# Joining the small matmuls behind z's sums, loading wo's last rows ahead of M's stores, and one normalisation behind an output block

## The chip, the cores and the metric

The kernel runs on one core of a Trainium2 chip. Five engines work side by side: TensorE (PE in the profile, its weight loads PEld), VectorE (DVE), ScalarE (ACT), GpSimd (POOL) and SyncE (SP), which here issues the DMAs. The metric is the device time of one execution in microseconds (us), as the median of repeated runs. For this kernel it was 301.76 us over three runs (301.67 to 302.19).

## The reference

The program mixes two blocks by a gate. Block A is a long convolution of the input along the sequence plus a skip term; block B is linear attention.

```python
x = A_u
g = _sigmoid((x * gate_w).sum(-1, keepdims=True))
a = _A_ref(x, A_A_re, A_A_im, A_B_re, A_B_im, A_C_re, A_C_im, A_log_dt, A_Dskip)
b = _B_ref(x, B_wqkv, B_wo)
return g * a + (1 - g) * b
```

Block B, with 32 heads of 20 channels, 2048 positions and 640 channels:

```python
phi = lambda t: jnp.where(t > 0, t + 1, jnp.exp(t)) + 1e-6
pq, pk = phi(q), phi(k)
kv = jnp.einsum("bhsd,bhse->bhde", pk, v)
z = jnp.einsum("bhsd->bhd", pk)
num = jnp.einsum("bhqd,bhde->bhqe", pq, kv)
den = jnp.einsum("bhqd,bhd->bhq", pq, z)[..., None] + 1e-6
o = num / den
return (lambda x, *d: x.transpose(*d))(o, 0, 2, 1, 3).reshape(B, S, D) @ wo
```

## The kernel before, in words

Each large product is made of three matmuls: an operand is split into a high part (`hi`, a copy on ScalarE) and a low part (`lo`, a subtraction on VectorE), and high by high, low by high and high by low are summed in PSUM (`mm3`).

**First stage (to about 146 us).** For 16 tiles of 128 positions the kernel computes k, its phi, the running sum `zacc`, and the product G = x^T phi(k), which is kept transposed in `GT` in five blocks of columns. Columns 512 to 640 come out turned the other way round, in the tile `rem`: two halves of 320 columns, copied out of PSUM at lines 610 (ScalarE) and 611 (VectorE).

**Second stage.** Everything here stands in the order of the string `PLAN`, read word by word by the loop at the end of `body`; each engine runs its instructions in the order in which they are written. The words are:

- `q`: one block of q for 512 positions and 128 channels, 15 matmuls into a PSUM tile `qp`, then exp, relu, phi (`qe`) and the denominator's running sum `acc` (`q_block`). Four groups of 512 positions have five blocks each.
- `z`: the denominator's constants (`z_const`, PSUM tile `cp`) and the gate's row (`gates_row`, PSUM tile `gp`).
- `kv0` to `kv2`: kv of a pair of head groups (a group has 120 channels, six heads) out of `GT` and the weights `Wv` (`kv_mm`, PSUM tile `kvps`). VectorE masks it into `kvT`, one of two tiles `kvz` that the pairs take in turn.
- `m0` to `m2`: M = kv times wo of a pair (`m_mm`, PSUM tiles `mps`), split into `Mgh` and `Mgl` and stored to DRAM. `ml` loads all of M back, reordered.
- `d`: the denominator of a group (`q_den`: PSUM tile `dp`, then a reciprocal).
- `n`: one block of q normalised (`q_norm`): VectorE multiplies `qe` by the denominator `d`; the high and low parts `pTh` and `pTl` follow with the next `flush`.
- `f`: one output block (`final_mm`: 15 matmuls into a PSUM tile `fp`; `final_out`: VectorE adds the convolution's part `yb` into `o`, which is stored). A `y_block` follows: a load of `yb`, or its computation, and a product with the gate on GpSimd.
- `c`: one convolution block (`conv_out`).

`z_part` (z's sums out of `zacc`, PSUM tile `zp`) stands ahead of the string. The five transposes of `rem` into `GT` (`rem_out`, PSUM tiles `tp`) stand behind the first `q`.

PSUM has eight banks: three with the tag `q`, three with the tag `f` (taken in turn by `kvps`, half of `mps`, `dp` and `fp`), two with the tag `m`. A tile is written anew only when its former content has been read. In SBUF the raw rows of `wo` of the groups 3 and 4 share the tag `wo`, with two slots; the last group's 40 rows (`wo_load(NB)`) take the slot of group 3, which is free when M of pair 1 has been computed. That load is asked for behind `m_mm(1)`, and so behind the eight stores of M that `m_mm(1)` issues on SyncE.

Of the kernel before, what the change touches and what calls it, by code (L numbers as in the profile page):

```python
# [30 lines left out]
F32 = mybir.dt.float32  # L31
# [8 lines left out]
P = 128  # L40
L = 2048
D = 640
NB = D // P
# [18 lines left out]


PLAN = """
q0 kv0 q0 z q0 m0 kv1 q0 c q0 m1 kv2
q1 d0 q1 m2 ml n0 q1 n0 n0 q1 n0 y q1 n0
q2 q2 y q2 d1 n1 f q2 n1 y f q2 n1 n1 f n1 f
q3 f q3 d2 n2 f q3 n2 f q3 n2 n2 f q3 n2 f
f d3 n3 f n3 n3 f n3 f n3 f
f f f f f f  # L70
"""
# [3 lines left out]
def f32(ap):  # L75
    return ap.bitcast(F32)


def body(tc, i, outT):
    nc = tc.nc  # L80
    pe, act, dve, pool, sp = nc.tensor, nc.scalar, nc.vector, nc.gpsimd, nc.sync
    outer, top, kst = ExitStack(), ExitStack(), ExitStack()

    def mk(stack, name, space=None):
        kw = {} if space is None else {"space": space}
        if space is not DRAM:
            kw["reuse_waits"] = "tile"
        return stack.enter_context(tc.tile_pool(name=name, bufs=1, **kw))
# [10 lines left out]
    def hi(dst, src):  # L99
        act.activation(dst, src, AF.Copy)  # L100

    def lo(dst, src, h, eng=None):
        (eng or dve).tensor_tensor(dst, src, f32(h), op=OP.subtract)  # L103
# [6 lines left out]
    def col(tag, n=NB, dt=F32):  # L110
        return pc.tile([P, n], dt, tag=tag, name=tag)
# [25 lines left out]
    s_all = col("s_all", NT)  # L137
    ident = col("ident", P)
    bdm = col("bdm", HC)
    kvz = [col(f"kvT{k}", P) for k in range(2)]  # L140
    for v in kvz:
        pool.memset(v, 0.0)
    dtc, k0, dsk, lam, ok = [col(n) for n in ("dtc", "k0", "dsk", "lam", "ok")]
# [74 lines left out]
    gps = {}  # L218
# [26 lines left out]
    def g_out(b, eng):  # L245
        src = gps.pop(b)
        (hi if eng is act else dve.tensor_copy)(GT[:, b, :512], src)


    kvs, wos = {}, {}  # L250


    def parts(gi):
        c0, n = GRP[gi]
        return [(r, c0 + o, min(HC, n - o)) for r, o in ((0, 0), (64, HC)) if o < n]

    def wo_load(gi):
        tag, nb = ("st", 3) if gi in (0, 1, 2) else ("wo", 2)
        w = wos[gi] = pw.tile([P, D + 2], F32, tag=tag, bufs=nb, name="wo")
        for r, c, n in parts(gi):  # L260
            m = min(64, D - c) if r == 0 else n
            sp.dma_start(w[r : r + m, :D], i["wo"][c : c + m, :])
# [3 lines left out]
    def out_row(gi, r):  # L266
        return r if gi % 2 == 0 else 64 - r

    def kv_mm(pr):
        p = pqp.tile([P, 512], F32, tag="f", bufs=3, name="kvps")  # L270
        kvT = kvs[pr] = kvz[pr % 2]
        for k, gi in enumerate((2 * pr, 2 * pr + 1)):
            for b in range(NB):
                for r, c, n in parts(gi):
                    pe.matmul(p[r : r + n, k * 64 : k * 64 + n], Wv[:, b, c : c + n], GT[:, b, c : c + n],
                              start=(b == 0), stop=(b == NB - 1))
        for k, gi in enumerate((2 * pr, 2 * pr + 1)):
            for r, c, n in parts(gi):
                o = out_row(gi, r)
                dve.tensor_tensor(kvT[r : r + n, o : o + n], p[r : r + n, k * 64 : k * 64 + n], bdm[r : r + n, :n],  # L280
                                  op=OP.mult)

    def m_mm(pr):
        kvT = kvs.pop(pr)
        both = 2 * pr, 2 * pr + 1
        ps = {}
        for hf in range(2):
            for gi in both:
                ps[gi, hf] = mbank("mps") if hf == 0 else pqp.tile([P, 512], F32, tag="f", bufs=3, name="mps")
            for gi in both:  # L290
                for r, c, n in parts(gi):
                    o = out_row(gi, r)
                    pe.matmul(ps[gi, hf][o : o + 64, :320], kvT[r : r + n, o : o + 64],
                              wos[gi][r : r + n, hf * 320 : hf * 320 + 320], start=True, stop=True,
                              tile_position=(r, o))
        for gi in both:
            wos.pop(gi)
            rows = slice(0 if len(parts(gi)) == 2 else out_row(gi, 0), P)
            h = pq.tile([P, D], F32R, tag="so", bufs=2, name="Mgh")
            l = pw.tile([P, D + 2], F32R, tag="st", bufs=3, name="Mgl")  # L300
            for hf in range(2):
                sl = slice(hf * 320, hf * 320 + 320)
                hi(h[rows, sl], ps[gi, hf][rows, :320])
                lo(l[rows, sl], ps[gi, hf][rows, :320], h[rows, sl])
            for v, to in ((h, M_d[0]), (l, M_d[1])):
                for r, c, m in parts(gi):
                    o = out_row(gi, r)
                    sp.dma_start(to[c : c + m, :], f32(v[o : o + m, :D]))
# [8 lines left out]
    def gates_row():  # L317
        gp = mbank("gp")
        pe.transpose(gp[:NT, :P], g, ident)
        gr = pc.tile([NT, P], F32, tag="gr", name="gr")  # L320
        dve.tensor_copy(gr, gp[:NT, :P])
        sp.dma_start(g_d, gr)
        for gi in range(NG):
            gb_load(gi)

    def z_part():

        zp = mbank("zp")
        for b in range(NB):
            pe.matmul(zp[:, b : b + 1], zacc[:, b * P : b * P + P], ones[:, :1], start=True, stop=True)  # L330
        dve.tensor_scalar(zc, zp[:, :NB], float(L) * EPS, None, op0=OP.add)
        dve.tensor_reduce(zs, zc, axis=AX.X, op=OP.add)
        z2 = zs.to_broadcast([P, 2])
        hi(zsh, z2)
        lo(zsl, z2, zsh)

    def z_const():
        cp = mbank("cp")
        pe.matmul(cp[:, :2], bm, zsh, start=True, stop=False)
        pe.matmul(cp[:, :2], bm, zsl, start=False, stop=True)  # L340
        dve.tensor_scalar(ch, cp[:, :1], EPS, EPS, op0=OP.mult, op1=OP.add)
# [60 lines left out]
    def u_load(j):  # L402
        gi, b = divmod(j, NB)
        if j < NK or j >= NS:
            us[j] = pw.tile([P, D + 2], F32, tag="st", bufs=3, name="u")
        else:
            us[j] = pq.tile([P, 512], F32, tag="u", bufs=1, name="u")
        sp.dma_start(us[j][:, :512], i["xT"][b * P : b * P + P, gi * 512 : gi * 512 + 512])
# [199 lines left out]
    g_main(NT - 1, (3, 4))  # L608
    rem = col("rem", D)
    hi(rem[:, :320], gps.pop(("r", 0))[:, :320])  # L610
    dve.tensor_copy(rem[:, 320:], gps.pop(("r", 1))[:, :320])
    g_out(3, act)
    g_out(4, dve)
    kst.close()
# [3 lines left out]
    pqp = mk(top, "pqp", PSUM)  # L618

    def mbank(name):  # L620
        return pqp.tile([P, 512], F32, tag="m", bufs=2, name=name)

    def rem_out():
        for b0, b1 in ((0, 4), (4, NB)):
            tp = mbank("tp")
            for b in range(b0, b1):
                pe.transpose(tp[:, (b - b0) * P : (b - b0 + 1) * P], rem[:, b * P : b * P + P], ident)
            hi(GT[:, b0:b1, 512:], tp[:, : (b1 - b0) * P].rearrange("p (b s) -> p b s", s=P))
# [50 lines left out]
    def q_norm(gi, b):  # L679
        e = qe.pop((gi, b))  # L680
        if b == 0:
            pqT[gi] = [px.tile([P, NB, 512], F32R, tag=f"x{c}{gi}", name=f"pT{c}{gi}") for c in "hl"]
        h, l = [v[:, b, :] for v in pqT[gi]]
        dve.scalar_tensor_tensor(e, e, EPS, rd[gi], op0=OP.add, op1=OP.mult)  # L684
        flush()
        pend.append((h, l, e))
# [39 lines left out]
    NJ = NG * NB  # L726
    n_q, n_n, n_f, n_y, n_c = 0, 0, 0, 0, NK
    z_part()
    if NS > NK:
        u_load(NK)  # L730
    for w in PLAN.split():
        what, k = w.rstrip("0123456789"), int("0" + w.lstrip("abcdefghijklmnopqrstuvwxyz"))
        if what == "q":
            q_block(*divmod(n_q, NB))
            n_q += 1
            if n_q == 1:
                rem_out()
        elif what == "z":
            z_const()
            gates_row()  # L740
        elif what == "d":
            q_den(k)
        elif what == "n":
            q_norm(*divmod(n_n, NB))
            n_n += 1
        elif what == "kv":
            kv_mm(k)
        elif what == "m":
            m_mm(k)
            if k == 1:  # L750
                wo_load(NB)
        elif what == "ml":
            m_load()
            for j in range(NS, min(NS + 3, NJ)):
                u_load(j)
        elif what == "c":
            conv_out(n_c)
            n_c += 1
            if n_c < NS:
                u_load(n_c)  # L760
        elif what == "y":
            y_block(n_y)
            n_y += 1
        elif what == "f":
            flush()
            final_mm(n_f)
            final_out(n_f)
            n_f += 1
            if n_y < NJ:
                y_block(n_y)  # L770
                n_y += 1
# [172 lines left out]
```

## Time and profile before

| what | value |
|---|---|
| median of three runs | 301.76 us |
| lowest and highest run | 301.67 and 302.19 us |
| profiled execution | 301.86 us |
| its span (first to last instruction) | 300.0 us |
| granted TensorE clock | 1.00 of full speed |
| bytes moved by DMA | 46.00 MB, 153 GB/s |

The profile is of one execution. In a row of the timeline the first number is the start in us from the span's start, the second the length in us, then come engine, line of the code, operation, output <- inputs, sizes and the number of merged instructions; in square brackets stands the idle time ahead of it and what ended that. In a row of the waits stand engine, tile and line, what it waited for, the us in total, how often, and the longest one. Matmuls are pipelined, so the length of one overlaps the next: how long TensorE is held is read from one start to the next start, not from lengths. Most q and output matmuls start 0.23 us apart.

### The profile page before, as it was taken

How to read it: one execution, taken by the hardware profiler on the slowest of the kernel's cores; microseconds unless marked ns; L12 is line 12 of the kernel's file. 1: busy time of each engine (PE TensorE's matmuls, PEld its weight loads, DVE VectorE, ACT ScalarE, POOL GpSimd, SP SyncE). 2: the span in 40 equal slices, each digit the busy share in tenths (PEclk: the TensorE clock that was granted, in tenths of full speed). 3: DMA queues.
4: the chain of work that ended last, by engine and by line, in shares of the span. 5: the costliest groups of instructions: out<-in, count | busy, mean ns of one | idle time of the engine just before them, and what ended most of it. 6: DMA issues, size and time to landing. Idle time of an engine off the chain costs nothing.

```text
span 300.0 us, 4539 instructions
## 1 busy us (share of the span) xinstructions
PE 294.0 (98%) x1627; PEld 255.3 (85%) x1627; DVE 230.7 (77%) x356; ACT 118.4 (39%) x249; POOL 46.5 (15%) x51
## 2 busy tenths in 40 slices
PE   8999999999999999999999999999999999999994
PEld 8998899999999999998887777888888888788884
DVE  2959976899899799956626679869685767888992
ACT  3565143444454345317343464551423233303100
POOL 3605330000000000000000000003232311243531
PEclk9999999999999999999999999999999999999999
DMA  6927285076767675381353653790326022135323
GB/s 183 314 67 228 81 256 177 12 218 183 252 185 236 215 203 188 101 252 46 91 158 107 238 178 108 238 348 31 105 71 193 19 86 64 62 140 179 120 91 110
DMA packets 28409, 46.00 MB, mean 153 GB/s; under 512 B 3771, under 2 KB 10827, under 8 KB 28383
## 3 DMA queue, kind: packets, MB, share of 16 engines
q1 hardware_dynamic: 28383, 45.66, 47.9%
q8 instruction: 15, 0.25, 0.3%
q14 instruction: 11, 0.09, 0.1%
HBM read 32.92 MB, written 12.72 MB: 152 GB/s over the span
## 4 chain that ended last, share of the span: by engine, by line
PE 89%; DVE 5%; issue 1%; ACT 1%; DMA 1%; SPq 1%; POOL 0%; DVEq 0%; ACTq 0%; POOLq 0%
PE fp L106 8%; PE fp L107 8%; PE fp L108 8%; PE qp L106 7%; PE qp L108 6%; PE qp L107 6%; PE k L107 6%; PE k L106 6%; PE k L108 6%; PE g L230 5%; PE g L228 5%; PE g L227 5%; PE g L452 4%; PE r L243 1%; PE r L242 1%
## 5 line engine op out<-in xcount | busy, mean ns | idle before, releaser
L437 POOL TENSOR_TENSOR yb<-yb,gb 128x512 f32<-128x512 f32 x20 | 29.3, 1469 | 218.9 <-DMA yb<-y_d 198.3
L106 PE MATMUL fp<-pTh,Mh 128*128 128x512 f32 (+1 forms) x105 | 39.9, 380 | 0.6 <-DVE o L723 0.6
L108 PE MATMUL fp<-pTl,Mh 128*128 128x512 f32 (+1 forms) x105 | 39.8, 379 | 0.0
L107 PE MATMUL fp<-pTh,Ml 128*128 128x512 f32 (+1 forms) x105 | 39.8, 379 | 0.0
L648 DVE SCALAR_TENSOR_TENSOR qe<-qe,qr 128x512 f32<-128x512 f32 x20 | 14.8, 742 | 23.0 <-ACT qr L645 23.0
L228 PE MATMUL g<-ph,xl 128*128 128x512 f32 x80 | 31.5, 394 | 0.0
L227 PE MATMUL g<-ph,xh 128*128 128x512 f32 x80 | 31.3, 392 | 0.0
L202 ACT ACTIVATE e<-k 128x320 f32<-128x320 f32 x25 | 10.9, 437 | 50.3 <-PE k L108 50.3
L100 ACT ACTIVATE pTh<-qe 128x512 fp32r<-128x512 f32 x20 | 12.6, 633 | 41.5 <-DVE qe L684 41.5
L206 DVE SCALAR_TENSOR_TENSOR e<-e,r 128x320 f32<-128x320 f32 x32 | 16.0, 505 | 13.7 <-ACT r L203 13.6
L230 PE MATMUL g<-pl,xh 128*128 128x512 f32 x80 | 26.1, 391 | 0.1
L106 PE MATMUL qp<-xTh,wqAh 128*128 128x512 f32 x60 | 23.9, 398 | 0.0
L106 PEld LDWEIGHTS fp<-pTh,Mh 128*128 128x128 f32 x105 | 19.7, 188 | 4.8 <-DVE o L723 1.1
L107 PE MATMUL qp<-xTh,wqAl 128*128 128x512 f32 x60 | 23.4, 390 | 0.0
L108 PE MATMUL qp<-xTl,wqAh 128*128 128x512 f32 x60 | 23.4, 390 | 0.0
L644 ACT ACTIVATE qe<-qp 128x512 f32<-128x512 f32 x20 | 11.9, 594 | 28.5 <-PE qp L108 24.7
L108 PEld LDWEIGHTS fp<-pTl,Mh 128*128 128x128 f32 x105 | 19.7, 188 | 3.8
L107 PEld LDWEIGHTS fp<-pTh,Ml 128*128 128x128 f32 x105 | 19.8, 188 | 3.7
L417 DVE TENSOR_TENSOR_SCAN y<-y,cY,zero 128x512 f32<-128x512 f32 x16 | 20.5, 1279 | 0.8 <-ACT y L416 0.8
L103 DVE TENSOR_TENSOR pTl<-qe,pTh 128x512 fp32r<-128x512 f32 x20 | 15.1, 763 | 6.8 <-ACT pTh L100 6.3
L107 PE MATMUL k<-wkAh,xTl 128*128 128x322 f32 x60 | 18.6, 310 | 0.0
L106 PE MATMUL k<-wkAh,xTh 128*128 128x322 f32 x60 | 18.6, 309 | 0.0
(169 smaller groups left out, 717.7 us busy)
## 6 DMA issues: line engine op xcount, KB each, us to landing
xraw<-in_x SPq DMA_DIRECT2D x16, 320.0 KB, 4.8
u<-in_xT SPq DMA_DIRECT2D x20, 256.0 KB, 5.6
out_T<-o SPq DMA_DIRECT2D x19, 256.0 KB, 2.6
y_d<-y SPq DMA_DIRECT2D x16, 256.0 KB, 2.3
yb<-y_d SPq DMA_DIRECT2D x16, 256.0 KB, 3.2
xTraw<-in_xTt SPq DMA_DIRECT2D x12, 320.0 KB, 4.6
Wv<-in_wv SPq DMA_DIRECT2D x5, 320.0 KB, 6.5
Mh<-M_dh SPq DMA_DIRECT2D x5, 320.0 KB, 4.6
```

Of the source, the lines that this page charges most:

```text
L100: act.activation(dst, src, AF.Copy)
L103: (eng or dve).tensor_tensor(dst, src, f32(h), op=OP.subtract)
L106: pe.matmul(out, ah, bh, start=start, stop=False)
L107: pe.matmul(out, al, bh, start=False, stop=False)
L108: pe.matmul(out, ah, bl, start=False, stop=stop)
L206: dve.scalar_tensor_tensor(e, e, 1.0, r[:, :n], op0=OP.min, op1=OP.add)
L227: pe.matmul(gps[b], xh[:, s], h[:, :512], start=t == 0, stop=False)
L228: pe.matmul(gps[b], xl[:, s], h[:, :512], start=False, stop=False)
L230: pe.matmul(gps[b], xh[:, b * P : b * P + P], l[:, :512], start=False, stop=t == NT - 1)
L417: dve.tensor_tensor_scan(y, y, zero.to_broadcast([P, 512]), cY[:, c], op0=OP.add, op1=OP.add)
L437: pool.tensor_tensor(ys[j], ys[j], gbs[j // NB], op=OP.mult)
L648: dve.scalar_tensor_tensor(e, e, 1.0, r, op0=OP.min, op1=OP.add)
```

## The change

Four edits, with what belongs to them:

1. `rem_out()` is called directly behind `z_part()` and no longer behind the first `q`. For that both halves of `rem` are copied by ScalarE, and the second transposes' tile comes from the tag `f` instead of `m`.
2. In `PLAN` the words `kv0 kv1 kv2` stand together behind `z`; `kvT` gets a third tile, and `m0`, `m1`, `m2` stand alone.
3. `wo_load(NB)` is issued inside `m_mm(1)`, behind its matmuls and ahead of its stores.
4. In the fourth row of `PLAN`, `n2 f` at the end becomes `f n2`: output block 8 stands ahead of the last normalisation of group 2.

```diff
-q0 kv0 q0 z q0 m0 kv1 q0 c q0 m1 kv2
+q0 z kv0 kv1 kv2 q0 q0 m0 q0 c q0 m1
 q1 d0 q1 m2 ml n0 q1 n0 n0 q1 n0 y q1 n0
 q2 q2 y q2 d1 n1 f q2 n1 y f q2 n1 n1 f n1 f
-q3 f q3 d2 n2 f q3 n2 f q3 n2 n2 f q3 n2 f
+q3 f q3 d2 n2 f q3 n2 f q3 n2 n2 f q3 f n2
 f d3 n3 f n3 n3 f n3 f n3 f
...
-    kvz = [col(f"kvT{k}", P) for k in range(2)]
+    kvz = [col(f"kvT{k}", P) for k in range(3)]
...
-        kvT = kvs[pr] = kvz[pr % 2]
+        kvT = kvs[pr] = kvz[pr]
...
         for gi in both:
             wos.pop(gi)
+        if pr == 1:
+            wo_load(NB)
+        for gi in both:
             rows = slice(0 if len(parts(gi)) == 2 else out_row(gi, 0), P)
...
-    dve.tensor_copy(rem[:, 320:], gps.pop(("r", 1))[:, :320])
+    hi(rem[:, 320:], gps.pop(("r", 1))[:, :320])
...
-            tp = mbank("tp")
+            tp = mbank("tp") if b0 == 0 else pqp.tile([P, 512], F32, tag="f", bufs=3, name="tp")
...
     z_part()
+    rem_out()
...
             n_q += 1
-            if n_q == 1:
-                rem_out()
...
             m_mm(k)
-            if k == 1:
-                wo_load(NB)
```

On TensorE, the transposes and the first kv stood between the first q block (PSUM tile `qp_1752`) and the second (`qp_1809`) before:

```order
L108 MATMUL qp_1752<-xTl0_130,wqAh_1617 128x512
L627 MATMUL tp_1775<-ident_98,rem_1727 128x128 x4
L627 MATMUL tp_1781<-ident_98,rem_1727 128x128
L275 MATMUL kvps_1784<-GT_120,Wv_121 60x60 x20
L106 MATMUL qp_1809<-xTh0_129,wqAh_1617 128x512
```

And now, at the same place between the first q block (`qp_1763`) and the second (`qp_1872`):

```order
L108 MATMUL qp_1763<-xTl0_132,wqAh_1619 128x512
L342 MATMUL cp_1786<-zsh_116,bm_118 128x2
L343 MATMUL cp_1786<-zsl_117,bm_118 128x2
L322 MATMUL gp_1790<-ident_98,g_111 16x128
L275 MATMUL kvps_1803<-GT_122,Wv_123 60x60 x20
L275 MATMUL kvps_1828<-GT_122,Wv_123 60x60 x20
L275 MATMUL kvps_1853<-GT_122,Wv_123 60x60 x10
L275 MATMUL kvps_1853<-GT_122,Wv_123 40x40 x5
L106 MATMUL qp_1872<-xTh0_131,wqAh_1619 128x512
```

The transposes have moved ahead of the first q block, the constants have come forward by one block, and the kv of the pairs 1 and 2, which stood behind `m0` and `m1`, have joined the first.

On SyncE, where the DMAs are issued in this order, the rows from the last convolution store (`y_d`) on were these before (`M_dh` and `M_dl` are M's two parts in DRAM; the four rows of stores, two DMAs each, are those of pair 1):

```order
L426 DMA y_d15_1953<-y_1949 128x512
L308 DMA M_dh_122<-Mgh_1993 60x640 x2
L308 DMA M_dl_123<-Mgl_1994 60x640 x2
L308 DMA M_dh_122<-Mgh_2003 60x640 x2
L308 DMA M_dl_123<-Mgl_2004 60x640 x2
L262 DMA wo_2013<-in_wo 40x640
```

And now:

```order
L429 DMA y_d15_1974<-y_1970 128x512
L262 DMA wo_2014<-in_wo 40x640
L311 DMA M_dh_124<-Mgh_2016 60x640 x2
L311 DMA M_dl_125<-Mgl_2017 60x640 x2
L311 DMA M_dh_124<-Mgh_2026 60x640 x2
L311 DMA M_dl_125<-Mgl_2027 60x640 x2
```

The 40 rows of `wo` have moved past the eight stores of pair 1.

On VectorE, around the last block of q (`accl` is the low part of group 3's denominator sum, `o` with `fp` an output block, `qe` with `d` a normalisation, `pTl` its low part), before:

```order
L103 TENSOR_TENSOR accl<-acc,acch 128x512
L684 SCALAR_TENSOR_TENSOR qe<-qe,d 128x512
L103 TENSOR_TENSOR pTl_2536<-qe,pTh_2535 128x512
L723 TENSOR_TENSOR o<-fp,yb 128x512 x2
L673 RECIPROCAL d<-d 128x512
```

And now:

```order
L103 TENSOR_TENSOR accl<-acc,acch 128x512
L726 TENSOR_TENSOR o<-fp,yb 128x512
L687 SCALAR_TENSOR_TENSOR qe<-qe,d 128x512
L103 TENSOR_TENSOR pTl_2538<-qe,pTh_2537 128x512
L726 TENSOR_TENSOR o<-fp,yb 128x512
L676 RECIPROCAL d<-d 128x512
```

The first of the two output blocks has moved ahead of the normalisation and its low part. TensorE's own order is the same there.

## The prediction

> **What bounds the kernel now.** I read the page's busy times and chain first, then TensorE's own waits, then the timeline of the stretches that the diff touches.
>
> ```profile
> span 300.0 us, 4539 instructions
> PE 294.0 (98%) x1627; PEld 255.3 (85%) x1627; DVE 230.7 (77%) x356; ACT 118.4 (39%) x249; POOL 46.5 (15%) x51
> PE 89%; DVE 5%; issue 1%; ACT 1%; DMA 1%; SPq 1%; POOL 0%; DVEq 0%; ACTq 0%; POOLq 0%
> PE mps L293 <- DMA wo<-in_wo: 0.3, 1, 0.3
> PE fp L106 <- DVE o L723: 0.6, 1, 0.6
> ```
>
> TensorE (PE) is busy in 98% of the span and carries 89% of the chain that ends last. So time can be won only where TensorE stands still, or where a matmul takes more than its pitch. Past the start-up TensorE has just the two waits in the last two rows: the third product of M waits for the last rows of `wo`, and one output block (`fp`) waits until VectorE (DVE) has read an older one. Both are places that the diff edits.
>
> **First wait: M of pair 2.**
>
> ```profile
> 178.46 0.39 PE L108 MATMUL qp<-xTl,wqAh 128*128 128x512 f32 x1
> 178.78 0.76 PE L293 MATMUL mps<-wo,kvT 60*64 60x320 f32 x4
> 179.86 1.26 PE L293 MATMUL mps<-wo,kvT 40*64 40x320 f32 x8 [0.33 <-DMA wo<-in_wo]
> 181.05 0.50 PE L106 MATMUL qp<-xTh,wqAh 128*128 128x512 f32 x1
> 159.44 1.31 PE L293 MATMUL mps<-wo,kvT 60*64 60x320 f32 x16
> 160.68 1.31 PE L275 MATMUL kvps<-GT,Wv 128*60 128x60 f32 x40
> ```
>
> The label says 0.33 us, but starts tell more. M of pair 2 holds TensorE from 178.78 to 181.05, 2.27 us for 12 records; M of pair 0, undisturbed, has 16 records and hands on after 160.68 - 159.44 = 1.24 us. Its matmuls on different corners of the array run side by side; in pair 2 the first four run alone, and the group that waited runs behind them. Without the wait pair 2 should take no longer than pair 0. I take 2.27 - 1.24 = **1.03 us**; the label's 0.33 us is the lower end.
>
> ```profile
> 168.96 1.31 PE L293 MATMUL mps<-wo,kvT 60*64 60x320 f32 x16
> 170.19 1.14 PE L275 MATMUL kvps<-GT,Wv 128*60 128x60 f32 x30
> 171.26 0.50 PE L106 MATMUL qp<-xTh,wqAh 128*128 128x512 f32 x1
> 176.91 0.30 SPq L262 DMA_DIRECT2D wo<-in_wo  x1
> ```
>
> The load is issued at 176.91, behind eight M stores, and was ready only about 3 us later. In the changed order SyncE issues it ahead of those stores, once M of pair 1 has read the slot that it reuses. M of pair 1 ended at 170.19 and now has kv 2 (1.07 us) ahead of it, so it ends about 0.85 later, near 171: the load goes out over 5 us earlier, with some 4 us to spare. The stores behind it wait for ScalarE and VectorE anyway, so the time that it takes on SyncE (0.30 us) is covered.
>
> **The gathering.** What is moved on TensorE keeps its count: 5 transposes and 110 kv records. Only switches and ends of blocks change.
>
> ```profile
> 150.23 0.71 PE L627 MATMUL tp<-ident,rem 128*128 128x128 f32 x5
> 150.87 1.31 PE L275 MATMUL kvps<-GT,Wv 128*60 128x60 f32 x40
> 152.11 0.50 PE L106 MATMUL qp<-xTh,wqAh 128*128 128x512 f32 x1
> 152.45 0.40 PE L107 MATMUL qp<-xTh,wqAl 128*128 128x512 f32 x1
> ```
>
> The first q matmul behind such a block holds 152.45 - 152.11 = 0.34 us, where q matmuls elsewhere stand 0.23 apart: 0.11 us for each return to q. There are six returns now (behind z's sums, kv 0, the constants, M 0 with kv 1, M 1 with kv 2, M 2) and five then: **0.11 us** won. Three kv blocks become one. 40 records take 152.11 - 150.87 = 1.24 us and 30 take 171.26 - 170.19 = 1.07 us, so a block has a part that doesn't grow with its records: between nothing (the 30 hold ten with one row part, which have no partner) and 0.56 us (a line through both points). Two of these ends go; I take 0.1 us each, near the low end as the slow ten explain most of it: **0.2 us**, bounds 0 and 1.1. The kv-to-q and M-to-kv hand-overs aren't seen apart in the trace, so both ends stay in the range.
>
> The Trainium skill, page "TensorEngine Tiling (Array Packing)", section "Key Properties", states that a change of tiling mode drains TensorE. By that rule alone every block that is joined saves a drain, and the sum would move toward the 1.1 end.
>
> Does anything new wait there?
>
> ```profile
> 144.62 0.46 ACT L100 ACTIVATE rem<-r 128x320 f32<-128x320 f32 x1
> 145.66 0.60 ACT L100 ACTIVATE GT<-g 128x512 f32<-128x512 f32 x1 [0.58 <-PE g L230]
> 146.72 0.48 PE L106 MATMUL qp<-xTh,wqAh 128*128 128x512 f32 x1
> 152.23 0.91 DVE L280 TENSOR_TENSOR kvT<-kvps,bdm 60x60 f32<-60x60 f32 x4
> 1.53 0.34 POOL L142 MEMSET kvT<- 128x128 f32 x2
> 4.40 0.98 POOL L103 TENSOR_TENSOR wkAl<-wraw,wkAh 128x322 fp32r<-128x322 f32 x1 [2.48 <-DVE wkAh L490]
> ```
>
> The transposes take the place of the q matmul at 146.72 and read both halves of `rem`. The second half goes from VectorE to ScalarE (ACT): 0.46 us from 145.08, inside the 0.58 us that ScalarE idles ahead of 145.66. It is done 1.2 us before it is read: nothing. ScalarE copies the transposes to `GT` while TensorE runs a whole q block (15 x 0.23 = 3.4 us) ahead of kv. The third `kvT` costs GpSimd (POOL) half of 0.34 us at the start, in front of 2.48 us of idling: nothing. Behind kv VectorE has eleven small products in one go, 11 x 0.91 / 4 = 2.5 us, while TensorE runs the next two q blocks; M 0 comes after those.
>
> One margin shrinks. M 0 and q's last blocks of group 0 now stand behind kv 2 as well, some 0.85 us later, and the denominator of group 0 doesn't.
>
> ```profile
> 170.91 0.75 DVE L654 SCALAR_TENSOR_TENSOR acc<-qe,zc,acc 128x512 f32<-128x512 f32 x1
> 172.42 0.69 DVE L103 TENSOR_TENSOR accl<-acc,acch 128x512 fp32r<-128x512 f32 x1 [0.76 <-ACT acch L100]
> 174.79 0.40 PE L669 MATMUL dp<-acch,bm 128*128 128x512 f32 x1
> ```
>
> `accl` ends at 173.11, 1.68 us before its reader at 174.79; with it 0.85 later and the reader about 0.25 earlier (the switches and ends saved by then) some 0.6 us are left. No wait, but it is the tightest new place.
>
> **Second wait: the output block at 261.65.**
>
> ```profile
> 257.21 0.69 DVE L103 TENSOR_TENSOR accl<-acc,acch 128x512 fp32r<-128x512 f32 x1 [0.76 <-ACT acch L100]
> 257.82 1.78 DVE L684 SCALAR_TENSOR_TENSOR qe<-qe,d 128x512 f32<-128x512 f32 x1
> 260.30 0.69 DVE L103 TENSOR_TENSOR pTl<-qe,pTh 128x512 fp32r<-128x512 f32 x1 [0.70 <-ACT pTh L100]
> 260.91 1.28 DVE L723 TENSOR_TENSOR o<-fp,yb 128x512 f32<-128x512 f32 x2
> 260.63 0.39 PE L670 MATMUL dp<-accl,bm 128*128 128x512 f32 x1
> 261.65 0.50 PE L106 MATMUL fp<-pTh,Mh 128*128 128x512 f32 x1 [0.64 <-DVE o L723]
> 257.42 1.63 POOL L437 TENSOR_TENSOR yb<-yb,gb 128x512 f32<-128x512 f32 x1 [6.02 <-DMA yb<-y_d]
> ```
>
> The `fp` at 261.65 needs the PSUM bank that VectorE frees with the first of the two `o` at 260.91; those stand behind a normalisation (257.82) and its low part (260.30). With the order turned, that first `o` follows `accl` at 257.9 and frees the bank three microseconds early. From 260.63 to 261.65 are 1.02 us for a pitch of 0.23: **0.79 us** go (the label says 0.64). What was ahead is now behind: the low part isn't needed until the block's thirteenth matmul, 12 x 0.23 = 2.8 us after its start, so it stays hidden.
>
> How much of the 0.79 reaches the end is set by the tail.
>
> ```profile
> 291.97 1.37 DVE L723 TENSOR_TENSOR o<-fp,yb 128x512 f32<-128x512 f32 x2
> 295.15 0.42 DVE L723 TENSOR_TENSOR o<-fp,yb 128x256 f32<-128x256 f32 x1 [1.81 <-DMA out_T<-o]
> 296.18 0.42 DVE L723 TENSOR_TENSOR o<-fp,yb 128x256 f32<-128x256 f32 x1 [0.61 <-PE fp L108]
> ```
>
> The last half block (296.18) waits for TensorE, but the half before it (295.15) waits for a store of VectorE's own output two blocks back, so for VectorE's line of work. If that line doesn't move against TensorE's, 295.57 is the floor: 296.18 - 295.57 = **0.61 us** of the 0.79 count. I cost VectorE's line at no change: the same instructions stand in it, and the 1.78 us of the normalisation is a collision with GpSimd's product (257.42 to 259.05) that the first `o` now partly fills. Ends: 0.79 if it gains 0.2, nothing if it loses 0.6.
>
> **Sum.** 1.03 + 0.11 + 0.2 + 0.61 = 1.95 us. The profiled execution took 301.86 us, its 300.0 us span and 1.86 us around it: 301.86 - 1.95 = **299.9 us**. The median shown is 301.76, 0.1 below it, inside its spread of 0.5.
>
> **Rivals.**
>
> *The tail takes the second gain back.* The loads of `yb` follow the stores of `o` on SyncE; an earlier `o` puts a GpSimd product against other VectorE work. The product for the next block would land near 262 beside the reciprocal, and the one behind it near 265.2, where this row stands:
>
> ```profile
> 265.56 0.69 DVE L676 TENSOR_TENSOR d<-d,og 128x512 f32<-128x512 f32 x1
> ```
>
> A collision costs up to 1.78 - 0.69 = 1.09 us. One that isn't made up uses the 0.61 up: 301.86 - 1.34 = 300.5. Against it: collisions that stand later in this line now would go.
>
> *The wait for `wo` was not all.* If M of pair 2 keeps most of its 2.27 us (banks, or the products that feed it), only the labelled 0.33 goes: 301.86 - 0.33 - 0.31 - 0.61 = 300.6. The even pace of pair 0 speaks against it.
>
> *Denominator of group 0 late.* If `accl` slips by 1.9 us instead of 0.85, TensorE stands 1.3 us at `dp`, which eats the first stage's gain; the rest is 0.61 or less: 301.2 to 301.8, no change within 0.2% (0.6 us), about what a measurement can tell.
>
> *Slower: VectorE's tail as the bound.* From 1.95 us of extra delay in VectorE's line after 258 all gains are gone, and each further us counts in full. That needs two collisions more than now (2.18 us); three give 301.86 - 1.95 + 3.27 = 303.2.
>
> ```profile
> 260.00:300.00 40.00, 35.51 (x170) 29.50 (x168) 31.41 (x34) 7.18 (x12) 13.62 (x9) 1.00 0.35 120
> ```
>
> For it: in the last 40 us (columns: busy time of PE, PEld, DVE, ACT, POOL) VectorE works 31.41 and GpSimd 13.62 us, so they must overlap. Against it: products that come earlier leave the later stretch freer by as much.
>
> The Trainium skill, page "SBUF — State Buffer", section "Who interferes with whom", states that a VectorE instruction with two SBUF inputs and a reading GpSimd one exclude each other for their whole length, and whichever comes first wins. By that rule the last rival is at its worst, as every product that comes first blocks. The trace agrees in the row at 257.82 (1.78 beside 0.69 us); no row shows how often it will happen then.
>
> **Chances.** Forecast 0.61 (299.3 to 300.4); tail takes the second gain 0.17; `wo` not all 0.10; denominator 0.07; slower 0.05. Faster by over 0.2% thus 0.88, within 0.2% 0.07, slower 0.05. The range 299.2 to 301.0 holds the first three, with the larger saving of the joined kv blocks at its low end.
>
> **What would show it.** Right: no idle time of M's matmuls for `wo`, its third block at 1.24 us; no wait of `fp` for `o` near 260; TensorE's last matmul about 2 us earlier, the last two half `o` nearly touching. Wrong: a wait at `dp` near 174.5, at the transposes near 146.7, or half an `o` at the end that waits for its store long after TensorE is done.

## The result, and the profile after

The changed kernel took 299.71 us as the median of five runs (299.24 to 300.06), the kernel before 301.67 us on the same chip (five runs, 301.39 to 302.19). The ratio is 0.993 with a 95% interval of 0.9917 to 0.9943, so the change saves between 1.7 and 2.5 us. The profiled execution took 299.84 us against 301.86 before.

The page of the changed kernel, for the span, the engines' busy time and the chain that ended last, answers to the first lines of the prediction:

```profile
span 298.1 us, 4538 instructions
PE 293.0 (98%) x1627; PEld 255.2 (86%) x1627; DVE 228.9 (77%) x355; ACT 119.0 (40%) x250; POOL 46.7 (16%) x52
PE 92%; DVE 3%; DMA 2%; issue 1%; ACT 1%; SPq 0%; DVEq 0%
```

TensorE is the bound as before, with 92% of the chain instead of 89%; VectorE's share fell from 5% to 3%. TensorE's waits in the changed kernel are down to one row, from the start-up:

```profile
PE k L131 <- POOL ones L122: 1.0, 1, 1.0
```

Neither `mps` nor `fp` stands in it. To see what each was worth, I measure from the start of z's sums (`zp`), where the edited part begins, since the first stage ahead of it is alike in both kernels and ends at slightly different times. The timeline of before, rows that the prediction didn't show:

```profile
145.69 1.17 PE L330 MATMUL zp<-ones,zacc 128*128 128x1 f32 x10
262.11 3.34 DVE L673 RECIPROCAL d<-d 128x512 f32<-128x512 f32 x1
269.20 1.78 DVE L684 SCALAR_TENSOR_TENSOR qe<-qe,d 128x512 f32<-128x512 f32 x2
295.86 0.28 PE L108 MATMUL fp<-pTl,Mh 128*128 128x256 f32 x1
```

The timeline of the changed kernel, from z's sums to M of pair 2:

```profile
146.15 1.17 PE L333 MATMUL zp<-ones,zacc 128*128 128x1 f32 x10
147.18 0.74 PE L630 MATMUL tp<-ident,rem 128*128 128x128 f32 x5
147.68 0.47 PE L106 MATMUL qp<-xTh,wqAh 128*128 128x512 f32 x1
151.53 3.34 PE L275 MATMUL kvps<-GT,Wv 128*60 128x60 f32 x110
154.80 0.50 PE L106 MATMUL qp<-xTh,wqAh 128*128 128x512 f32 x1
172.16 0.30 SPq L262 DMA_DIRECT2D wo<-in_wo  x1
173.53 0.69 DVE L103 TENSOR_TENSOR accl<-acc,acch 128x512 fp32r<-128x512 f32 x1 [0.76 <-ACT acch L100]
174.82 0.40 PE L672 MATMUL dp<-acch,bm 128*128 128x512 f32 x1
178.80 1.30 PE L293 MATMUL mps<-wo,kvT 60*64 60x320 f32 x12
180.03 0.50 PE L106 MATMUL qp<-xTh,wqAh 128*128 128x512 f32 x1
```

M of pair 2 is one undivided row now and holds TensorE for 180.03 - 178.80 = 1.23 us instead of 2.27. All twelve take about as long as the eight that waited took by themselves before (181.05 - 179.86 = 1.19 us), so the first four cost next to nothing when they run beside them. The load that it waited for goes out at 172.16 instead of 176.91. From `zp` to the q matmul behind M of pair 2 are 180.03 - 146.15 = 33.88 us, where before had 181.05 - 145.69 = 35.36: 1.48 us saved, 1.04 of them at M and 0.44 by the gathering. `accl` ends at 174.22. The `dp` row at 174.82 is the product of `acch`; that of `accl` starts at 175.05, 0.83 us behind the end of `accl`.

The second place, and the end, in the changed kernel's timeline:

```profile
256.35 1.66 POOL L440 TENSOR_TENSOR yb<-yb,gb 128x512 f32<-128x512 f32 x1 [4.59 <-DMA yb<-y_d]
256.78 0.68 DVE L726 TENSOR_TENSOR o<-fp,yb 128x512 f32<-128x512 f32 x1
257.38 1.18 DVE L687 SCALAR_TENSOR_TENSOR qe<-qe,d 128x512 f32<-128x512 f32 x1
259.58 0.39 PE L673 MATMUL dp<-accl,bm 128*128 128x512 f32 x1
259.81 0.39 PE L106 MATMUL fp<-pTh,Mh 128*128 128x512 f32 x1
260.74 3.35 DVE L676 RECIPROCAL d<-d 128x512 f32<-128x512 f32 x1 [0.19 <-ACT d L675]
267.84 1.28 DVE L687 SCALAR_TENSOR_TENSOR qe<-qe,d 128x512 f32<-128x512 f32 x2
293.28 0.43 DVE L726 TENSOR_TENSOR o<-fp,yb 128x256 f32<-128x256 f32 x1 [1.88 <-DMA out_T<-o]
293.92 0.28 PE L108 MATMUL fp<-pTl,Mh 128*128 128x256 f32 x1
294.23 0.42 DVE L726 TENSOR_TENSOR o<-fp,yb 128x256 f32<-128x256 f32 x1 [0.53 <-PE fp L108]
```

The output block follows `dp` at the pitch, 259.81 - 259.58 = 0.23 us, where 1.02 us stood. `o` goes ahead, and the normalisation behind it takes 1.18 us instead of 1.78. From `zp` to TensorE's last matmul are 293.92 - 146.15 = 147.77 us; before it was 295.86 - 145.69 = 150.17. So 2.40 us are saved, 1.48 up to M of pair 2 and 0.92 after it. The last two half `o` still stand apart (293.71 to 294.23): VectorE waits for TensorE at the very end, as before.

### The profile page after: what moved, and what is told of

Its sections match the earlier page's. It is cut to its first block, busy times and chain, and to the rows that moved or that the text cites. A ratio compares the mean times of both kernels' runs of the same rounds, so it can differ in the third digit from the quotient of the medians.

```text
span 298.1 us, 4538 instructions
## 1 busy us (share of the span) xinstructions
PE 293.0 (98%) x1627; PEld 255.2 (86%) x1627; DVE 228.9 (77%) x355; ACT 119.0 (40%) x250; POOL 46.7 (16%) x52
## 4 chain that ended last, share of the span: by engine, by line
PE 92%; DVE 3%; DMA 2%; issue 1%; ACT 1%; SPq 0%; DVEq 0%
PE qp L106 8%; PE fp L108 8%; PE fp L107 8%; PE fp L106 8%; PE qp L108 8%; PE qp L107 8%; PE k L107 6%; PE k L106 6%; PE k L108 6%; PE g L230 5%; PE g L228 5%; PE g L227 5%; PE g L455 3%; DMA wraw<-in_wkB 2%; PE r L242 1%; PE r L243 1%
## 5 line engine op out<-in xcount | busy, mean ns | idle before, releaser
L440 POOL TENSOR_TENSOR yb<-yb,gb 128x512 f32<-128x512 f32 x20 | 28.4, 1423 | 217.5 <-DVE acc L657 157.7
L651 DVE SCALAR_TENSOR_TENSOR qe<-qe,qr 128x512 f32<-128x512 f32 x20 | 15.4, 770 | 21.5 <-ACT qr L648 21.5
L103 DVE TENSOR_TENSOR pTl<-qe,pTh 128x512 fp32r<-128x512 f32 x20 | 16.1, 819 | 6.8 <-ACT pTh L100 6.3
```

The costliest lines, as they stand in the source:

```text
L440: pool.tensor_tensor(ys[j], ys[j], gbs[j // NB], op=OP.mult)
L651: dve.scalar_tensor_tensor(e, e, 1.0, r, op0=OP.min, op1=OP.add)
```

## The experiments

Two theories had to be told apart at each place: that each edit brings its own term of the sum, or that the saving comes from some of them, or from them together. In each experiment I compare TensorE from `zp` to its last matmul (150.17 us before, 147.77 changed) and the times of repeated runs. Before's median in the runs beside the first four kernels is 301.82 us.

**The load of wo's last rows alone** (`e1_wo`).

```diff
         for gi in both:
             wos.pop(gi)
+        if pr == 1:
+            wo_load(NB)
+        for gi in both:
...
             m_mm(k)
-            if k == 1:
-                wo_load(NB)
```

> Before, with wo's last rows asked for ahead of M's stores and nothing else. My theory (the starts of the matmuls): M of pair 2 falls from 2.27 us to about 1.24 us, TensorE's last matmul and the time come 1.0 us earlier. Rival (the label of the wait): only the labelled 0.33 us goes, M of pair 2 stays near 1.9 us. Second rival (covered): no change in the time, since something else stops TensorE soon after.

Its timeline at M of pair 2:

```profile
179.65 1.30 PE L293 MATMUL mps<-wo,kvT 60*64 60x320 f32 x12
180.88 0.50 PE L106 MATMUL qp<-xTh,wqAh 128*128 128x512 f32 x1
```

Again 1.23 us in one row. `zp` to the last matmul is 149.14 us, 1.03 less than before. The median is 301.04 us, ratio 0.9962 (0.9947 to 0.9978). The label on the waiting row named 0.33 us, and three times as much was won: the label tells only how long nothing ran, not that two groups which share the array ran one behind the other. The median fell by 0.78 us.

**The normalisation behind the output block alone** (`e2_fn`).

```diff
-q3 f q3 d2 n2 f q3 n2 f q3 n2 n2 f q3 n2 f
+q3 f q3 d2 n2 f q3 n2 f q3 n2 n2 f q3 f n2
```

> Before, with output block 8 ahead of the last normalisation of group 2 and nothing else. The record's sum: the wait of 0.79 us goes, 0.61 us of it reaches the end because VectorE's line in the tail doesn't move. What the trace of the changed kernel suggests instead: VectorE's line comes forward by as much as TensorE, so 0.8 to 0.9 us reach the end and the last half block waits for TensorE, not for a store. Rival (collisions): VectorE's line gets later, the time stays within 0.3 us.

The end of its timeline on VectorE:

```profile
293.82 0.42 DVE L723 TENSOR_TENSOR o<-fp,yb 128x256 f32<-128x256 f32 x1 [1.88 <-DMA out_T<-o]
294.68 0.42 DVE L723 TENSOR_TENSOR o<-fp,yb 128x256 f32<-128x256 f32 x1 [0.44 <-PE fp L108]
```

TensorE is 1.07 us shorter (149.10); M of pair 2 happened to take 0.15 less in this execution, so 0.92 belong to the edit, as in the changed kernel. The last two `o` keep 0.44 us between them, so the tail didn't catch the gain in this execution. The median is 301.21 us, 0.61 less than before, ratio 0.9972 (0.9956 to 0.9989).

**The gathering alone** (`e3_gather`): `rem_out` forward with what belongs to it, three `kvT`, the first row of the plan; wo's load stays behind the stores.

```diff
-q0 kv0 q0 z q0 m0 kv1 q0 c q0 m1 kv2
+q0 z kv0 kv1 kv2 q0 q0 m0 q0 c q0 m1
...
-    kvz = [col(f"kvT{k}", P) for k in range(2)]
+    kvz = [col(f"kvT{k}", P) for k in range(3)]
...
     z_part()
+    rem_out()
```

> Before, with the gathering alone (transposes behind z's sums, kv of all pairs together, three kvT, both halves of rem on ScalarE); wo's last rows stay behind M's stores. If the edits are independent: 0.3 to 0.45 us faster. If they hang together, as I think: M of pair 1 and so its stores and the load behind them come about 0.85 us later, while M of pair 2 comes 0.3 to 0.45 us earlier, so M of pair 2 grows from 2.27 to about 3.5 us, which takes more than the gathering gives: 0.5 to 0.9 us slower.

Its timeline at the issue of wo's load and M of pair 2:

```profile
178.36 0.29 SPq L262 DMA_DIRECT2D wo<-in_wo  x1
178.39 0.76 PE L293 MATMUL mps<-wo,kvT 60*64 60x320 f32 x4
181.13 1.26 PE L293 MATMUL mps<-wo,kvT 40*64 40x320 f32 x8 [1.99 <-DVE d L673]
182.32 0.50 PE L106 MATMUL qp<-xTh,wqAh 128*128 128x512 f32 x1
```

This alone is slower: `zp` to the last matmul is 151.38 us (1.21 more), the median of six runs 304.46 us, ratio 1.0079 (1.0049 to 1.0108). M of pair 2 starts 178.39 - 145.73 = 32.66 us behind `zp`, 0.43 earlier than before (33.09), so the gathering's own saving is there. But M of pair 1 and its eight stores now come later, and so does the load behind them, 178.36 instead of 176.91. M of pair 1 starts 0.65 us later behind `zp` (169.65 - 145.73 against 168.96 - 145.69), the load goes out 1.41 later. M of pair 2 holds TensorE 3.93 us instead of 2.27, more than the 3.5 expected. The median lost more than TensorE did in this profile, which is of the fastest of the six runs; three of the six had a mean clock of 0.991 to 0.993 and are the three longest (last section). The label names VectorE's `d`; the load, issued 2.77 us ahead of that row, was ready at the same time, as it was 2.95 us behind its issue before. The experiment `e11_nowo` settles which it was.

**The third `kvT` alone** (`e4_kvt`).

```diff
-    kvz = [col(f"kvT{k}", P) for k in range(2)]
+    kvz = [col(f"kvT{k}", P) for k in range(3)]
...
-        kvT = kvs[pr] = kvz[pr % 2]
+        kvT = kvs[pr] = kvz[pr]
```

> Before, with a third kvT tile (one more 128x128 memset on GpSimd at the start) and nothing else. The first stage of the changed kernel ended 0.46 us later in its profile (z's sums at 146.15 instead of 145.69). If that is the scatter of the first loads: no change of the median (within 0.3 us), z's sums at 145.7 to 146.2 whichever kernel. Rival: the memset (or the moved tiles) delays the first stage: 0.4 us slower, z's sums at 146.1 or later.

The median is 302.10 us, ratio 1.0006 (0.999 to 1.0022): nothing, and `zp` starts at 145.44, no later than before (145.69). The later `zp` of the changed kernel's profile is thus not this edit's. But its profile had no wait at the output block, though the order there is before's. TensorE needs 149.17 us from `zp` there, 1.00 less than before, 0.24 of it at M of pair 2 (2.03 us instead of 2.27). The profile is of the fastest of the twelve runs. GpSimd, VectorE and TensorE at that place:

```profile
257.33 0.69 DVE L684 SCALAR_TENSOR_TENSOR qe<-qe,d 128x512 f32<-128x512 f32 x1
257.46 1.71 POOL L437 TENSOR_TENSOR yb<-yb,gb 128x512 f32<-128x512 f32 x1 [6.54 <-DVE accl L103]
260.38 0.50 PE L106 MATMUL fp<-pTh,Mh 128*128 128x512 f32 x1
```

GpSimd's product came 0.13 us behind the normalisation, which then took 0.69 us. In before it came 0.40 us ahead (257.42 against 257.82), and the normalisation took 1.78. So the second wait may hang on which of the two comes first.

**The changed kernel again** (`e6_after`), without an edit, beside the three that follow; before's median there is 301.92 us.

> The changed kernel once more, as the reference of the next three and to see what scatters. From z's sums to TensorE's last matmul it took 147.77 us (before 150.17). Expected again within 0.1 us, since no wait is left in it; the first stage before it scatters by some 0.5 us (z's sums at 145.3 to 146.6 in six profiles). Rival: the stretch itself scatters, as the old one did.

The median is 299.69 us, ratio 0.9923 (0.9905 to 0.994), and TensorE again needs 147.77 us from `zp`. `zp` starts at 145.75 here and at 146.15 in the first profile. VectorE's line isn't the same:

```profile
264.53 1.70 DVE L687 SCALAR_TENSOR_TENSOR qe<-qe,d 128x512 f32<-128x512 f32 x1
293.62 0.76 DVE L726 TENSOR_TENSOR o<-fp,yb 128x256 f32<-128x256 f32 x2 [1.89 <-DMA out_T<-o]
```

GpSimd's product starts 0.15 us ahead of the normalisation behind the reciprocal (264.38 against 264.53), which takes 1.70 us; in the first profile the normalisation came 0.11 us ahead of the product and took 0.69. VectorE's line slips by that, and the last two half `o` follow each other without a gap, behind the wait for a store. The last one ends 294.38 - 145.75 = 148.63 us behind `zp`, against 148.50 in the first profile and 150.91 before: the tail binds here, and it costs 0.13 us.

**The changed kernel with the old fourth row** (`e7_nofn`).

```diff
-q3 f q3 d2 n2 f q3 n2 f q3 n2 n2 f q3 f n2
+q3 f q3 d2 n2 f q3 n2 f q3 n2 n2 f q3 n2 f
```

> The changed kernel with the last normalisation of group 2 ahead of output block 8 again. My theory now: the old wait is a race. If GpSimd's product starts before that normalisation, the latter takes 1.8 us and the output block waits 0.8 us (1.02 us between matmuls); if VectorE comes first, it takes 0.69 us and there is no wait, as in the kernel with only the third kvT. So the profile shows one of the two, z's sums to the last matmul take 147.8 or 148.7 us, and the median is 0.4 to 0.9 us over that of the changed kernel. Rival (a fixed wait of the order): always 1.02 us, always 0.9 us slower. Rival (tail): no difference in the time.

Its timeline at the output block:

```profile
256.33 1.30 POOL L440 TENSOR_TENSOR yb<-yb,gb 128x512 f32<-128x512 f32 x1 [4.98 <-DMA yb<-y_d]
256.37 1.80 DVE L687 SCALAR_TENSOR_TENSOR qe<-qe,d 128x512 f32<-128x512 f32 x1
260.21 0.50 PE L106 MATMUL fp<-pTh,Mh 128*128 128x512 f32 x1 [0.65 <-DVE o L726]
260.55 0.39 PE L107 MATMUL fp<-pTh,Ml 128*128 128x512 f32 x1
```

Wait and long normalisation are back with GpSimd only 0.04 us ahead. TensorE is 0.91 us longer (148.68), the median is 300.73 us, ratio 0.996 (0.9945 to 0.9976): 1.04 us above the changed kernel's 299.69. On TensorE the fourth row is worth its 0.9 us with the other edits as without; by medians it is 1.04 and 0.61. All six runs lie between 300.60 and 300.92, so nothing in their times shows an escape from the wait, and by this experiment alone it could be a fixed one; `e4_kvt` shows that it isn't.

**The kv blocks apart again** (`e8_split`), all else as changed.

```diff
-q0 z kv0 kv1 kv2 q0 q0 m0 q0 c q0 m1
+q0 z kv0 q0 kv1 q0 m0 q0 kv2 c q0 m1
```

> The changed kernel with the three kv apart again, each between two q blocks (kv 0, q, kv 1, q, M 0, q, kv 2). From the two profiles: three separate blocks took 1.24 + 1.25 + 1.07 = 3.56 us, the joined one 3.27, and a return to q costs 0.11: 0.29 + 2 x 0.11 = 0.5 us more from z's sums to the last matmul (148.3 us). Rival (each change of the array's tiling drains it, some 0.35 to 0.5 us as at M): 0.8 us or more. Rival (the count of matmuls alone decides): no difference.

Its timeline around one of the three blocks:

```profile
155.79 0.39 PE L108 MATMUL qp<-xTl,wqAh 128*128 128x512 f32 x1
156.11 1.31 PE L275 MATMUL kvps<-GT,Wv 128*60 128x60 f32 x40
157.35 0.50 PE L106 MATMUL qp<-xTh,wqAh 128*128 128x512 f32 x1
```

TensorE is 0.78 us longer (148.55); the median is 300.94 us, ratio 0.9967 (0.9954 to 0.998). The blocks take 1.25, 1.24 and 1.07 us, 3.56 together, where the joined one takes 154.80 - 151.53 = 3.27: 0.29 us. Going into a block costs 156.11 - 155.79 = 0.32 us where q matmuls stand 0.23 apart, so 0.09, and coming out 0.11. Two more ways in and out are 0.40, and 0.69 of the 0.78 are accounted for. The 0.5 expected was too small, since it left out the way in: each block apart costs about 0.39 us (0.78 / 2), which is the size that the rival named. By medians the splitting costs 1.25 us (300.94 against 299.69).

**kv ahead of everything** (`e9_front`): the joined block directly behind the transposes, without a q block between.

```diff
-q0 z kv0 kv1 kv2 q0 q0 m0 q0 c q0 m1
+kv0 kv1 kv2 z q0 q0 q0 m0 q0 c q0 m1
```

> One step further: kv of all pairs directly behind the transposes, then the constants, then the q blocks. It saves one return to q and, if the joined pieces overlap as those did, 0.1 to 0.3 us: 147.5 to 147.7 us from z's sums to the last matmul. Rival: kv now waits for what it reads, VectorE's copy of the last block of G (it ended at 147.4, kv would start at 147.7) or ScalarE's copies of the transposes (148.6, the third kv would start at 150): 0.3 us or more lost, seen as a wait of TensorE at kv.

```profile
147.31 0.74 PE L630 MATMUL tp<-ident,rem 128*128 128x128 f32 x5
147.98 3.34 PE L275 MATMUL kvps<-GT,Wv 128*60 128x60 f32 x110
151.25 0.27 PE L342 MATMUL cp<-zsh,bm 128*128 128x2 f32 x1
```

In these rows of its timeline kv stands 0.67 us behind the start of the transposes, where q stands 0.50 behind it in the changed kernel, and takes 3.27 us as there. TensorE needs 147.79 us, the median is 300.20, ratio 0.994 (0.9923 to 0.9956). The 0.1 to 0.3 us expected were not won, and no wait at kv, as the rival had it, appeared: where the joined block stands makes no difference that TensorE shows.

**GpSimd's product moved away, the order of before kept** (`e10_race`). The `yb` load and product that collided are issued earlier, at a new word `y`, and no longer behind the output block ahead of the collision.

```diff
-q3 f q3 d2 n2 f q3 n2 f q3 n2 n2 f q3 n2 f
+q3 f q3 d2 n2 f y q3 n2 f q3 n2 n2 f q3 n2 f
...
-            if n_y < NJ:
+            if n_y < NJ and n_f != 8:
```

> Before, with one product of GpSimd taken out from beside the normalisation: the load and product that follow output block 7 are issued two blocks earlier, behind block 5; every VectorE and TensorE instruction stays in its place. If the second wait is the collision: the normalisation ahead of output block 8 takes 0.69 us instead of 1.78, TensorE's 1.02 us in front of the next block fall to 0.23 and z's sums to the last matmul fall from 150.17 to about 149.3 us; the time falls by 0.4 to 0.9 us, less than that if the runs of before mostly escape the collision. Rival (the order alone makes the wait): the 1.02 us stay, and so does the time.

Its timeline on VectorE, at the normalisation, at the one behind the reciprocal and at the end:

```profile
258.00 0.68 DVE L684 SCALAR_TENSOR_TENSOR qe<-qe,d 128x512 f32<-128x512 f32 x1
266.14 1.67 DVE L684 SCALAR_TENSOR_TENSOR qe<-qe,d 128x512 f32<-128x512 f32 x1
294.30 0.69 DVE L723 TENSOR_TENSOR o<-fp,yb 128x512 f32<-128x512 f32 x1 [1.32 <-DMA out_T<-o]
295.45 0.75 DVE L723 TENSOR_TENSOR o<-fp,yb 128x256 f32<-128x256 f32 x2 [0.46 <-PE fp L108]
```

Without a product beside it the normalisation takes 0.68 us, and TensorE has no wait there: 149.21 us from `zp`, 0.96 less than before. So the second wait came from that collision; the turned order of the changed kernel takes the release of the PSUM bank out from behind it. But the collision moved on: the normalisation at 266.14 takes 1.67 us instead of 0.69 (266.28 before), with GpSimd's next product 0.27 us ahead of it (265.87). The same normalisation takes 1.67 us in `e4_kvt` too (265.48). And at the end a whole `o` now waits for the store of an older one (1.32 us idle), the two half `o` follow it back to back, and the last `o` ends only 0.63 us earlier behind `zp` than before. The runs don't show even that: median 301.76 us against 301.82, ratio 0.9994 (0.9982 to 1.0006). In this profile the tail takes a third of TensorE's gain; the runs show none of the gain, where 0.4 to 0.9 us were expected. In the profile of `e2_fn`, with the swap in the plan, the normalisation behind the reciprocal takes 0.69 us (265.37) and the tail doesn't bind.

**The changed kernel with wo's load back behind the stores** (`e11_nowo`).

```diff
         for gi in both:
             wos.pop(gi)
-        if pr == 1:
-            wo_load(NB)
...
             m_mm(k)
+            if k == 1:
+                wo_load(NB)
```

> The changed kernel with wo's last rows behind M's stores again. As in the gathering alone, M of pair 2 should grow from 1.23 to about 3.9 us: z's sums to the last matmul 147.8 + 2.7 = 150.5 us. If that is all, the time is 299.7 + 2.7 = 302.4 us. If so long a stop of TensorE also lowers its clock for a while, as the gathering alone suggests (its runs at a mean clock of 0.991 to 0.993 took 1.5 us more than those at 0.997), the median is 303 us or more, and the slow ones show the lower clock. Rival (edits independent): 300.7 us, as before lost 1.03 us at this place.

The row of the granted clock on its page (tenths of full speed, 40 slices of 7.6 us), and its timeline at M of pair 2:

```profile
PEclk9999999999999999999999995999999999999999
178.34 0.29 SPq L262 DMA_DIRECT2D wo<-in_wo  x1
181.04 1.76 PE L293 MATMUL mps<-wo,kvT 40*64 40x320 f32 x8 [1.80 <-DMA wo<-in_wo]
183.75 0.63 PE L108 MATMUL qp<-xTl,wqAh 128*128 128x512 f32 x1
184.18 0.63 PE L106 MATMUL qp<-xTh,wqAh 128*128 128x512 f32 x1
```

The median of ten runs is 302.90 us, ratio 1.0036 (1.0011 to 1.0062), 3.2 us above the changed kernel. That lies between the 302.4 expected of the wait alone and the 303 expected with a slower clock; the rival of independent edits (300.7) is out. In this profile `zp` to the last matmul takes 153.46 us, 3.0 more than the 150.5 expected, because of the clock (last section). Here the label names the load itself, issued and ready at the same times as in the gathering alone, so that one's `d` was a coincidence. The reciprocal that writes `d` runs here to 181.22 (177.87 + 3.35), and M goes on at 181.04 without waiting for it. Taken out of the whole, wo's edit costs three times the 1.03 us that it won by itself: 2.7 us if M of pair 2 takes what it took in the gathering alone (3.93 - 1.23), and in some executions a slower clock on top (last section).

## Why the prediction was right, point by point

The forecast of 299.9 us stands 0.2 above the median, inside the runs. Its terms held less well than its sum.

| term | predicted | measured behind `zp` |
|---|---|---|
| M of pair 2 | 1.03 | 1.04 (alone: 1.03) |
| gathering: return to q, joined kv | 0.31 | 0.44 |
| second wait, what reaches the end | 0.61 | 0.92 |
| sum | 1.95 | 2.40 |

The profiled executions differ by 301.86 - 299.84 = 2.02 us only, because the first stage of after's happened to end 0.46 us later (`zp` at 146.15 against 145.69; over the twelve profiles it starts between 145.27 and 146.56). The medians differ by 1.96 and, in the repeat, by 2.23. So the terms were undersized by up to 0.45 us together, and part of the close hit is luck: the 2.40 us compare two profiles, and in `e4_kvt` before's order took 1.00 us less on TensorE than in before's own profile.

- **First wait: right, size and cause.** Starts of matmuls gave 1.03, the label 0.33. The load went out 4.75 us earlier; that was ample.
- **Gathering: right in sign, a little small.** The joined kv saves 0.29 us (1.24 + 1.25 + 1.07 - 3.27), where I took 0.2; the transposes hold 0.50 instead of 0.64 (not predicted); one return to q saves 0.11. That makes 0.54, and 0.44 were seen; the difference lies in other hand-overs, such as 0.20 us from the gate's row to kv (151.33 to 151.53), and wasn't split further. The splitting of kv shows that each switch has its price, 0.09 in and 0.11 out. The Trainium skill's statement that a change of tiling mode drains TensorE (page "TensorEngine Tiling (Array Packing)", section "Key Properties") agrees in kind; at 0.2 us for a switch there and back it didn't move the sum to the upper end of 1.1 us. With what is lost inside the blocks, a block apart costs 0.39 us in `e8_split`, where the upper end of 1.1 us assumes 0.56; what the price consists of, no run shows.
- **The margin at the denominator: no wait, as predicted, but read off the wrong row.** 0.6 us were predicted up to the row at 174.79, and 0.60 are measured up to its counterpart at 174.82; both rows read `acch`. The matmul that reads `accl` starts at 175.03 before and at 175.05 now, so the margin was 1.92 us and is 0.83.
- **Second wait on TensorE: right, slightly small.** 0.92 us after M of pair 2 against the 0.79 predicted; I took the stop itself less one pitch, while the first `fp` behind such a stop also holds TensorE longer (260.55 - 260.21 = 0.34 us in `e7_nofn`, not 0.23). The stop need not be long for that: in `e4_kvt`, where no wait is shown, the same `fp` holds TensorE 0.33 us too.
- **The tail: the mis-sized term.** I let 0.61 us through, as VectorE's line would not move, and left the rest of the 0.79 to a floor at 295.57. VectorE's line did move. The reciprocal stood 262.11 - 145.69 = 116.42 us behind `zp` and now stands 260.74 - 146.15 = 114.59 behind it, 1.83 earlier; the half `o` that waits for a store moved from 149.46 to 147.13, 2.33 earlier. That is 0.85 beyond the 1.48 of the first stage, so the floor came forward with TensorE's end. Two shorter collisions are seen in it: the normalisation at 1.18 instead of 1.78 us, and the pair of normalisations behind the reciprocal at 1.28 (267.84) instead of 1.78 (269.20). So the last two half `o` stood 0.52 us apart, where the prediction had them nearly touching. In the repeat `e6_after` they do touch: there the half `o` that waits for a store comes 147.87 us behind `zp`, only 0.11 beyond the 1.48, and the end gains 0.13 less. The floor itself exists: it bound there and in `e10_race`, where TensorE gained 0.96 us and its last `o` only 0.63.
- **The rivals.** None shows in the changed kernel's first profile. The first rival's product landed at 261.06, beside the reciprocal, as foreseen, and did no harm (the reciprocal took 3.35 us, 3.34 before). The product behind it, foreseen near 265.2, did collide in the repeat `e6_after` (1.70 us at 264.53), but the tail took back 0.13 us and not 0.61. In `e10_race` a tail took more, and in `e3_gather` and `e11_nowo` a wait for `wo` grew. The price of the third rival was worked out wrong: by its own figures a slip of 1.9 us, with the reader 0.25 earlier, leaves TensorE waiting for 1.9 + 0.25 - 1.68 = 0.47 us, not 1.3.
- **What the prediction missed: the edits hang together.** I added them up as if each stood alone. Alone, the gathering loses 2.6 us of median: it delays M of pair 1 and the stores in front of wo's load, which costs TensorE 1.21 us in its profile, and in half of its runs the clock was lower as well. By medians the three single edits add up to -0.78 - 0.61 + 2.64 = +1.25 us, and all of them together give -1.96. With wo's load ahead of the stores that price is gone.

Still open is why `e10_race` gains nothing over its runs while its one profile shows 0.63 us (the collision that moved on fits the third that is missing there, not the rest), and how often before's own executions escape the collision as that of `e4_kvt` did.

## What to carry to other kernels

Read the price of a wait from the starts of the matmuls around it, against an undisturbed block of the same kind, not from the waiting row's label. Before work is moved ahead of a step, look at what is queued behind that step's DMAs: here the gathering paid only once the load of `wo` stood ahead of the stores. A gain on TensorE near the end is worth what the eviction line behind it can follow, so see whether the line's own collisions go, stay or move on. One profile shows one outcome of a race: here a second profile of the same kernel showed the other.

## What the runs showed of the hardware

**A race of two engines made the second wait.** The normalisation on VectorE has two SBUF inputs, GpSimd's product reads SBUF. GpSimd started first, by 0.40 us in before and by 0.04 in `e7_nofn`, and the normalisation took 1.78 and 1.80 us; in `e4_kvt` VectorE was first by 0.13 us and took 0.69, and GpSimd 1.71. So 0.17 us in the order of arrival decide over a wait of about 1 us on a third engine. The Trainium skill, page "SBUF — State Buffer", section "Who interferes with whom", says that two such instructions exclude each other for their whole length and that the order of issue decides; these rows agree. In the changed kernel `o` at 256.78, whose one input `fp` lies in PSUM, ran its 0.68 us beside GpSimd's product unhindered, and the normalisation behind it waited only for the rest.

**A stop of TensorE can cost the clock.** In the profile of `e11_nowo` TensorE idled 1.80 us, and from 183.32 on twelve q matmuls stood 0.43 us apart (183.75 to 184.18) instead of 0.23; the granted clock was 0.50 from 184 to 188 us, and its mean over the span 0.989. Against `e3_gather`, whose profile has 1.99 us of idling at the same place and no such drop, the q block takes 6.21 us instead of 3.54 and the second part of M 1.69 instead of 1.19: 3.17 us together. Of the ten runs of `e11_nowo` the two longest (305.24 and 305.99 us) are the two with a mean clock of 0.989; the four with 1.000 took 302.50 to 303.13. Of the six runs of `e3_gather` the three longest (304.68 to 305.79) are those with 0.991 to 0.993. No run of a kernel without the long stop has a mean clock below 0.995. What makes the drop come in one execution and not in the next, no run shows. The Trainium skill, page "TensorE: Matmul & The Clock Gate", section "Part 1: The HAM clock gate (the "warmup" mystery)", gives half rate after at least one idle window of about 3.4 us, in windows that run freely. That the drop comes in some executions only would fit the free windows, and 0.43 is about twice 0.23; but here 1.80 us of idling were enough, and the measurement decides.
